# Attention with two expert layers: GpSimd carries the pairwise sums of raw keys and values one step further

## The chip, the cores and the metric

The kernel runs on one core of a Trainium2 chip. The metric is the device time of one execution in microseconds (us); the kernel before took 1105.7 us (median of 3 runs, 1105.57 to 1106.48). Lower is better. The engines are TensorE (PE), VectorE (DVE), ScalarE (ACT), GpSimd (POOL) and SyncE (SP), which here only issues transfers.

## The reference, cut to what matters

```python
# q, k, v: (8 batches, 8 heads, 576 rows, 64), float32
k_p = k.reshape(B, H, 72, 8, D).mean(axis=3)        # eight raw rows -> one
v_p = v.reshape(B, H, 72, 8, D).mean(axis=3)
scores = (q @ k_p.transpose(0, 1, 3, 2)) / sqrt(D)
attn = softmax(scores)
x = (attn @ v_p)                                     # 4608 tokens x 512
x = moe(x, w_gate, w_output_gate, w1, w2)            # 8 experts, best one per token
x = moe2(x, modality_id, w_gate, modality_bias, w1, w2)
```

The part that the change touches is the mean over eight raw rows of keys and of values, of which each batch has one tensor apiece.

## The kernel before

The 4608 tokens are worked off in 36 tiles of 128. A batch has 576 tokens, so a tile takes in the end of one batch and the start of the next now and then. The attention stage fills the first 170 us of the span; the two expert stages behind it take the rest, and the change leaves them alone.

Raw keys (or values) of a batch lie on chip as eight planes of 128 partitions x 288 numbers, where plane p holds the p-th of each eight rows. They come in two transfers of four planes, each into one buffer of a ring of seven (`ring`, names kv0 to kv6). The sum of the eight planes is built as a tree, in three places:

- `half` (L304): on GpSimd, for each of the two buffers, two additions of one plane each (L307, 128x288), which leave two planes per buffer.
- `both` (L311): on VectorE, one addition of two planes to two planes (L313, 128x576), and one of the two planes left (L315, 128x288). Behind L313 the second buffer goes back to the ring.
- `spread` (L317): ScalarE copies the sum, scaled, into the layout that the matmuls read (L327: KB for keys, VT for values). Then the first buffer goes back.

The first batch is summed on VectorE in a way of its own. In iteration i of the tile loop the program issues, engine by engine: eviction of the transposed weights of tile i-2 (`stage_et_evict`, L408, ScalarE); scores of tile i (L380, PE); the products with the values for tile i-2 (`stage_av`, L417, PE, into pav); row maxima of tile i (L385, VectorE) and their exponentials (L392, ScalarE); one entry of `lasts`, that is a `both` or a `spread`; `normalise` of tile i-2 (L431 to L438, VectorE, which reads pav); transposes of tile i-1 (L401, PE). Between these VectorE takes single steps of a list `fill` (L471 to L488): the choice of experts for a finished group of four tiles, many short instructions on 128x32 numbers or fewer, most with two inputs on chip. Twelve such steps more (L128 to L139) follow once the fourth group is through. GpSimd's work is put in order by `gp_work` (L497 and L307): each call takes one `half`, if its transfers have been issued, and one scatter of a finished tile to DRAM. Each engine works its instructions off in the order of the program.

There is one buffer of pav, so the products of the next tile wait for `normalise` of the one before. The transfers are issued on SP in the order of the program (`ldq`); one that finds no free buffer at build time makes the program issue an open sum first (`advance`), and at run time it waits for the last reader of its buffer.

Of the kernel before, what the change touches and what calls it, by code (L numbers as in the profile page):

```python
# [14 lines left out]
ALU = mybir.AluOpType  # L15
AX = mybir.AxisListType
# [26 lines left out]
SCALE = 1.0 / (8.0 * POOL)  # L43
# [4 lines left out]
def kernel(ctx, tc, q, k, v, wg, wo, w1, w2, mod, wg2, bias2, v1, v2, out):  # L48
    nc = tc.nc
    PE, ACT, DVE, GP, SP = nc.tensor, nc.scalar, nc.vector, nc.gpsimd, nc.sync  # L50
# [220 lines left out]
    KB = [pa.tile([P, NG, 2, SP_], F32, name=f"KB{i}", bufs=1) for i in range(3)]  # L271
    VB = [pa.tile([CB, NB, 2 * VW], F32, name=f"VB{i}", bufs=1) for i in range(3)]
    VT = [pa.tile([P, NG, 2, SP_], F32, name=f"VT{i}", bufs=1) for i in range(2)]
# [5 lines left out]
    qT, kR, vR = {}, {}, {}  # L279
# [19 lines left out]
                    SP.dma_start(t[lo], src[b, :, lo:lo + 4])  # L299
                ldq.append((tag, load))  # L300

    def pool_sum(eng, first, raw, dst, scale):
        def half(lo, eng):
            r = raw[lo]  # L304
            if eng is GP:
                for j in range(2):
                    GP.tensor_tensor(r[:, j], r[:, j], r[:, 2 + j], op=ALU.add)  # L307
            else:
                eng.tensor_tensor(r[:, 0:2], r[:, 0:2], r[:, 2:4], op=ALU.add)

        def both():  # L311

            DVE.tensor_tensor(raw[0][:, 0:2], raw[0][:, 0:2], raw[4][:, 0:2], op=ALU.add)  # L313
            ring.append(raw[4])
            DVE.tensor_tensor(raw[0][:, 2], raw[0][:, 0], raw[0][:, 1], op=ALU.add)  # L315

        def spread():  # L317
            apart_heads(dst, raw[0][:, 2], slice(0, NG), scale)
            ring.append(raw[0])

        return [lambda: half(0, first), lambda: half(4, eng)], [both, spread]

    def apart_heads(dst, x, gs, scale):

        for r in range(2):
            h = slice(64 * r, 64 * r + 64)
            ACT.activation(dst[h, gs, r, :], x[h].rearrange("p (g s) -> p g s", s=SP_), AF.Copy, scale=scale)  # L327

    def sum_k(b, eng):
        return pool_sum(eng, eng, kR.pop(b), KB[b % 3], SCALE)  # L330

    def sum_v(b, eng, first=None):
        return pool_sum(eng, first or eng, vR.pop(b), VT[b % 2], 1.0)

    def prep_v(b, a, name="pv"):
        t = VT[b % 2].rearrange("p g r s -> p (g r s)")
# [7 lines left out]
    def cols(T):  # L344
        t0, r0, res = T * P, 0, []
        while r0 < P:
            b = (t0 + r0) // S
            s0 = (t0 + r0) % S
            n = min(P - r0, S - s0)
            res.append((b, s0, r0, n))  # L350
            r0 += n
        return res
# [152 lines left out]
    ring = [kp.tile([P, 4, KW], F32, name=f"kv{i}") for i in range(KV)]  # L505
# [14 lines left out]
    def prefetch(b):  # L520
        load_kv(b)
        for tag, (f, l) in ((b, sum_k(b, GP)), (b + 0.1, sum_v(b, GP))):
            sums.extend((tag, g) for g in f)
            lasts.extend((tag, g) for g in l)
# [60 lines left out]
    for i in range(3):  # L585
        o = VB[i].rearrange("p (a j) (r c) -> p a j r c", a=2, r=2)
# [19 lines left out]
    kR.pop(0)  # L606
    ring.extend(k0)
    v0 = [f for fs in sum_v(0, DVE, GP) for f in fs]
    v0.pop(0)()

# [14 lines left out]
    late, vbs = [], []  # L625
# [36 lines left out]
    for i in range(NT + 1):  # L662
# [76 lines left out]
        if i + 2 < NT:  # L739
            b = cols(i + 2)[-1][0]  # L740
# [470 lines left out]
```

## Time and profile before

| what | value |
|---|---|
| median of 3 runs | 1105.7 us (1105.57 to 1106.48) |
| the profiled execution's own time | 1104.66 us |
| its span | 1103.0 us |
| granted TensorE clock, mean | 0.993 |
| busy over the span | PE 97%, DVE 54%, ACT 36%, POOL 29% |

The profiled execution is one more run; its trace covers 1103.0 us of its 1104.66 us. A busy share over the whole span mixes the attention stage, where VectorE and ScalarE are busy most of the time, with the expert stages, where they are not. For this change only the first 170 us are to be read.

### The profile page before, as it was taken

To read this page: it belongs to the slowest core of one execution; us is meant where nothing else is said; L and a number is where in the kernel's file an instruction comes from. 1 tells how busy PE (TensorE), PEld (TensorE's weight loads), DVE (VectorE), ACT (ScalarE), POOL (GpSimd) and SP (SyncE) were. 2 spreads that over 40 slices of the span, in tenths; PEclk is the share of its full clock that TensorE was granted. 3 is DMA by queue.
4 is the path that set the end of the run, shared out by engine and by line. 5 is a ranking of instruction groups with operands and counts; after the bars stand their busy time and mean duration, and the time that the engine had idled before them with its cause. 6 is when DMAs were issued, how large, how long until landed. Compare 5 with 4: busy or idle time off the path is not lost. (4 is left out here: it accounts for less than half of the span.)

```text
span 1103.0 us, 21979 instructions
## 1 busy us (share of the span) xinstructions
PE 1066.7 (97%) x7058; PEld 962.2 (87%) x7058; DVE 594.2 (54%) x1845; ACT 393.4 (36%) x924; POOL 324.9 (29%) x551
## 2 busy tenths in 40 slices
PE   7998989999999999999999999999999999999997
PEld 6998878998889888888898887988899889998886
DVE  6889777767888668669766685121111221121111
ACT  6887882215455125235312251121111332221121
POOL 7666485112847214316611111001010050000010
PEclk9999999999999999999999999999999999999999
DMA  9877455613737213316250013711111111111000
GB/s 346 283 279 259 176 178 216 216 55 109 249 131 244 77 49 135 104 40 193 76 186 24 22 42 138 240 49 43 56 50 40 41 52 48 40 40 41 30 30 23
DMA packets 52099, 128.20 MB, mean 116 GB/s; under 512 B 6957, under 2 KB 10029, under 8 KB 51760
## 3 DMA queue, kind: packets, MB, share of 16 engines
q1 hardware_dynamic: 42928, 97.28, 26.9%
q0 software_dynamic: 8960, 28.47, 6.6%
q8 instruction: 89, 1.46, 0.6%
q14 instruction: 122, 1.00, 0.3%
HBM read 92.51 MB, written 34.27 MB: 115 GB/s over the span
## 5 line engine op out<-in xcount | busy, mean ns | idle before, releaser
L773 DVE SCALAR_TENSOR_TENSOR hl<-h,hh 128x512 fp32r<-128x512 f32 x140 | 95.3, 690 | 367.5 <-ACT hh L772 365.2
L827 PE MATMUL y<-W2H,hh 128*128 128x512 f32 x608 | 234.3, 398 | 2.1 <-ACT hh L772 1.5
L827 PE MATMUL y<-W2L,hh 128*128 128x512 f32 x608 | 233.9, 395 | 0.5 <-POOL W2L L841 0.5
L827 PE MATMUL y<-W2H,hl 128*128 128x512 f32 x608 | 232.4, 395 | 0.0
L772 ACT ACTIVATE hh<-h 128x512 fp32r<-128x512 f32 x140 | 83.2, 596 | 308.0 <-PE h L783 304.5
L850 DVE CUSTOM_DVE_ANT_0 junk<-y,wg2b 128x512 f32<-128x512 f32 x273 | 169.5, 685 | 8.3 <-ACTq L1054 5.1
L830 ACT ACTIVATE y<-y,xg 128x512 f32<-128x512 f32 x76 | 52.3, 688 | 303.4 <-PE y L827 224.1
L1075 POOL DMA_INDIRECT out_dram<-y,ti x37 | 36.0, 972 | 381.4 <-ACT y L830 259.3
L827 PEld LDWEIGHTS y<-W2H,hh 128*128 128x128 f32 x608 | 114.1, 189 | 27.8 <-ACT hh L772 1.7
L827 PEld LDWEIGHTS y<-W2H,hl 128*128 128x128 f32 x608 | 114.5, 188 | 26.7
L827 PEld LDWEIGHTS y<-W2L,hh 128*128 128x128 f32 x608 | 114.6, 189 | 25.9 <-POOL W2L L841 1.3
L783 PE MATMUL h<-xH,W1L 128*128 128x256 f32 x608 | 123.0, 284 | 0.0
L841 POOL TENSOR_TENSOR W2L<-R,W2H 128x256 fp32r<-128x256 f32 x128 | 91.8, 753 | 78.7 <-ACT W2H L1056 76.9
L904 POOL DMA_INDIRECT xs<-y,qdi x39 | 39.8, 1021 | 218.5 <-DVE lg L850 160.6
L783 PE MATMUL h<-x2H,W1L 128*128 128x256 f32 x512 | 103.6, 284 | 0.0
L783 PE MATMUL h<-xH,W1H 128*128 128x256 f32 x608 | 100.2, 288 | 1.3 <-ACTq L1054 0.8
L783 PE MATMUL h<-xL,W1H 128*128 128x256 f32 x608 | 98.2, 284 | 0.0
L783 PEld LDWEIGHTS h<-xH,W1L 128*128 128x128 f32 x608 | 95.3, 193 | 0.0
L783 PEld LDWEIGHTS h<-xH,W1H 128*128 128x128 f32 x608 | 84.4, 193 | 1.7 <-ACTq L1054 1.2
L783 PE MATMUL h<-x2H,W1H 128*128 128x256 f32 x512 | 84.5, 287 | 0.4 <-ACT x2H L245 0.4
L783 PEld LDWEIGHTS h<-xL,W1H 128*128 128x128 f32 x608 | 84.3, 193 | 0.0
L783 PE MATMUL h<-x2L,W1H 128*128 128x256 f32 x512 | 83.0, 284 | 0.3 <-DVE x2L L252 0.2
(240 smaller groups left out, 1596.3 us busy)
## 6 DMA issues: line engine op xcount, KB each, us to landing
R<-in_w_dram SPq DMA_DIRECT2D x56, 512.0 KB, 5.1
xg<-xs SPq DMA_DIRECT2D x72, 258.0 KB, 2.7
kv<-in_v_dram SPq DMA_DIRECT2D x16, 576.0 KB, 5.8
R<-in_v_dram SPq DMA_DIRECT2D x16, 512.0 KB, 8.5
kv<-in_k_dram SPq DMA_DIRECT2D x14, 576.0 KB, 6.7
qt<-in_q_dram SPq DMA_DIRECT2D x14, 576.0 KB, 9.0
xs<-dummy SPq DMA_DIRECT2D x18, 258.0 KB, 2.7
wraw<-in_w_dram SPq DMA_DIRECT2D x8, 512.0 KB, 4.1
```

Of the source, the lines that this page charges most:

```text
L772: ACT.activation(HH[kk], p, AF.Relu)
L773: DVE.scalar_tensor_tensor(HL[kk], in0=p, scalar=0.0, in1=HH[kk].bitcast(F32), op0=ALU.max, op1=ALU.subtract)
L783: PE.matmul(p[:, c2, :], lhsT=W[d][:, c:c + P], rhs=x[:, d, :], start=n == 0, stop=n == 3 * ND - 1)
L827: PE.matmul(p, lhsT=X[f // 2][:, f % 2, hf * P:(hf + 1) * P], rhs=W[f // 2][:, f % 2, :], start=i == 0, stop=i == 3 * NF - 1)
L830: ACT.activation(S["y"][:, hf, 0:DM], p, AF.Copy, scale=S["xg"][:, hf, DM:DM + 1])
L841: GP.tensor_tensor(W2L[j][:, c, w], R2[j][:, c, w], W2H[j][:, c, w].bitcast(F32), op=ALU.subtract)
L850: DVE.tensor_tensor_reduce(out=M["junk"][:, e % 2], in0=p, in1=M["wg2b"][:, e, :], scale=1.0, scalar=0.0, op0=ALU.mult, op1=ALU.add, accum ...
L904: apart("xs2", GP.indirect_dma_start(xs2, IDX(ap=di[:, hf:hf + 1], axis=0), y[:, hf, :], None, bounds_check=E * REG - 1, oob_is_err=False))
L1075: apart("out", GP.indirect_dma_start(out, IDX(ap=S["ti"][:, hf:hf + 1], axis=0), S["y"][:, hf, 0:DM], None, bounds_check=N - 1, oob_is_err ...
```

## The change

From the third batch on (`late`, b > 1), GpSimd adds the second buffer's four planes into planes 2 and 3 of the first buffer, and then adds planes 2 and 3 to planes 0 and 1: six additions of 128x288 for a tensor instead of four. VectorE sums the two planes left by one `tensor_reduce` over a view in which the two numbers to be added stand side by side (they lie 288 numbers apart), instead of two `tensor_tensor`. For the first two batches the additions stay as they were, but the second buffer's result is written into the first buffer too. For all batches the second buffer goes back to the ring behind `half`, no longer behind `both`, so the ring hands out other buffers, and at one place a `both` that the program had to issue early is now issued later.

```diff
--- before.py
+++ after.py
@@ -299,19 +299,26 @@
                     SP.dma_start(t[lo], src[b, :, lo:lo + 4])
                 ldq.append((tag, load))
 
-    def pool_sum(eng, first, raw, dst, scale):
+    def pool_sum(eng, first, raw, dst, scale, late):
         def half(lo, eng):
-            r = raw[lo]
+            r, o = raw[lo], raw[0][:, lo // 2:lo // 2 + 2]
             if eng is GP:
                 for j in range(2):
-                    GP.tensor_tensor(r[:, j], r[:, j], r[:, 2 + j], op=ALU.add)
+                    GP.tensor_tensor(o[:, j], r[:, j], r[:, 2 + j], op=ALU.add)
             else:
-                eng.tensor_tensor(r[:, 0:2], r[:, 0:2], r[:, 2:4], op=ALU.add)
+                eng.tensor_tensor(o, r[:, 0:2], r[:, 2:4], op=ALU.add)
+            if lo:
+                ring.append(r)
+                if late:
+                    for j in range(2):
+                        GP.tensor_tensor(raw[0][:, j], raw[0][:, j], raw[0][:, 2 + j], op=ALU.add)
 
         def both():
 
-            DVE.tensor_tensor(raw[0][:, 0:2], raw[0][:, 0:2], raw[4][:, 0:2], op=ALU.add)
-            ring.append(raw[4])
+            if late:
+                DVE.tensor_reduce(raw[0][:, 2], raw[0][:, 0:2].rearrange("p j c -> p c j"), axis=AX.X, op=ALU.add)
+                return
+            DVE.tensor_tensor(raw[0][:, 0:2], raw[0][:, 0:2], raw[0][:, 2:4], op=ALU.add)
             DVE.tensor_tensor(raw[0][:, 2], raw[0][:, 0], raw[0][:, 1], op=ALU.add)
 
         def spread():
@@ -327,10 +334,10 @@
             ACT.activation(dst[h, gs, r, :], x[h].rearrange("p (g s) -> p g s", s=SP_), AF.Copy, scale=scale)
 
     def sum_k(b, eng):
-        return pool_sum(eng, eng, kR.pop(b), KB[b % 3], SCALE)
+        return pool_sum(eng, eng, kR.pop(b), KB[b % 3], SCALE, b > 1)
 
     def sum_v(b, eng, first=None):
-        return pool_sum(eng, first or eng, vR.pop(b), VT[b % 2], 1.0)
+        return pool_sum(eng, first or eng, vR.pop(b), VT[b % 2], 1.0, b > 1)
 
     def prep_v(b, a, name="pv"):
         t = VT[b % 2].rearrange("p g r s -> p (g r s)")
```

On VectorE, in the third and fourth iteration: nm are the row maxima, rs to lgs are `normalise`, kv_198 is the buffer with the second batch's keys. Before:

```order
L385 TENSOR_REDUCE nm_389<-ps_373 128x4
L313 TENSOR_TENSOR kv_198<-kv_198,kv_199 128x576
L315 TENSOR_TENSOR kv_198<-kv_198 128x288
L431 TENSOR_SCALAR rs<-pav 128x8
L433 RECIPROCAL rs<-rs 128x8
L435 TENSOR_TENSOR x<-pav,rs 128x512
L436 TENSOR_TENSOR ll<-pav,rs 128x128
L438 TENSOR_REDUCE lgs<-ll 128x16
L385 TENSOR_REDUCE nm_444<-ps_431 128x4
```

The same place after the change (its line numbers are 7 or 8 higher):

```order
L392 TENSOR_REDUCE nm_389<-ps_373 128x4
L438 TENSOR_SCALAR rs<-pav 128x8
L440 RECIPROCAL rs<-rs 128x8
L442 TENSOR_TENSOR x<-pav,rs 128x512
L443 TENSOR_TENSOR ll<-pav,rs 128x128
L445 TENSOR_REDUCE lgs<-ll 128x16
L321 TENSOR_TENSOR kv_198<-kv_198 128x576
L322 TENSOR_TENSOR kv_198<-kv_198 128x288
L392 TENSOR_REDUCE nm_446<-ps_433 128x4
```

The sum of the second batch's keys stands behind the first `normalise` now, and right ahead of the next row maxima.

On VectorE at the sum of the seventh batch's keys, among the twelve steps on the expert counts (fe to ford). Before:

```order
L385 TENSOR_REDUCE nm_1624<-ps_1607 128x4
L132 TENSOR_SCALAR feh_308<-rev,fm_307 128x8
L313 TENSOR_TENSOR kv_195<-kv_195,kv_194 128x576
L315 TENSOR_TENSOR kv_195<-kv_195 128x288
L133 TENSOR_TENSOR ft_309<-feh_308,ev 128x8
L431 TENSOR_SCALAR rs<-pav 128x8
L134 TENSOR_REDUCE fef_310<-ft_309 128x1
```

After:

```order
L392 TENSOR_REDUCE nm_1636<-ps_1619 128x4
L132 TENSOR_SCALAR feh_308<-rev,fm_307 128x8
L319 TENSOR_REDUCE kv_198<-kv_198 128x288
L133 TENSOR_TENSOR ft_309<-feh_308,ev 128x8
L438 TENSOR_SCALAR rs<-pav 128x8
L134 TENSOR_REDUCE fef_310<-ft_309 128x1
```

Two instructions have become one, at the same place in the row.

On GpSimd around the sums of the sixth batch, where xs is the scatter of a finished tile and each row of sums is two additions. Before:

```order
L307 TENSOR_TENSOR kv_198<-kv_198 128x288 x2
L497 DMA xs_66<-x,rdi 37888x516
L307 TENSOR_TENSOR kv_197<-kv_197 128x288 x2
L497 DMA xs_66<-x,rdi 37888x516
L427 COPY x<-meta 128x4x3
L307 TENSOR_TENSOR kv_200<-kv_200 128x288 x2
L307 TENSOR_TENSOR kv_199<-kv_199 128x288 x2
L497 DMA xs_66<-x,rdi 37888x516 x2
```

After:

```order
L307 TENSOR_TENSOR kv_194<-kv_194 128x288 x2
L504 DMA xs_66<-x,rdi 37888x516
L307 TENSOR_TENSOR kv_194<-kv_199 128x288 x2
L314 TENSOR_TENSOR kv_194<-kv_194 128x288 x2
L504 DMA xs_66<-x,rdi 37888x516
L434 COPY x<-meta 128x4x3
L307 TENSOR_TENSOR kv_196<-kv_196 128x288 x2
L307 TENSOR_TENSOR kv_196<-kv_197 128x288 x2
L314 TENSOR_TENSOR kv_196<-kv_196 128x288 x2
L504 DMA xs_66<-x,rdi 37888x516 x2
```

Two more additions stand in one run behind each second `half`: runs of two become runs of four, and the run of four for the values becomes one of six.

## Rows read from the trace of the kernel before

**Rows 1.** Windows: us, busy of each engine (instructions), clock, DMA share, GB/s.

```profile
20.00:96.00 76.00, 73.29 (x594) 69.74 (x594) 65.70 (x210) 61.15 (x222) 47.26 (x58) 1.00 0.84 301
96.00:126.00 30.00, 24.77 (x202) 22.91 (x201) 27.86 (x88) 20.75 (x76) 15.50 (x20) 1.00 0.65 221
```

**Rows 2.** Waits of PE, 30 to 126 us: total us, times, longest.

```profile
PE pav L417 <- DVE ll L436: 3.2, 2, 1.8
PE pav L417 <- ACT et L408: 1.9, 6, 0.6
PE pav L417 <- DVE ra L477: 1.1, 1, 1.1
```

**Rows 3.** Timeline of PE: start, us, what, [idle before <-releaser].

```profile
102.40 1.89 PE L417 MATMUL pav<-VB,et 96*128 96x162 f32 x12 [1.76 <-DVE ll L436]
...
121.06 1.89 PE L417 MATMUL pav<-VB,et 96*128 96x162 f32 x12 [1.45 <-DVE ll L436]
```

**Rows 4.** Timeline of VectorE at three of the sums.

```profile
81.30 0.75 DVE L313 TENSOR_TENSOR kv<-kv,kv 128x576 f32<-128x576 f32 x1
82.08 0.46 DVE L315 TENSOR_TENSOR kv<-kv 128x288 f32<-128x288 f32 x1
82.85 0.17 DVE L431 TENSOR_SCALAR rs<-pav 128x8 f32<-128x8 f32 x1 [0.31 <-PE pav L417]
...
98.06 0.77 DVE L313 TENSOR_TENSOR kv<-kv,kv 128x576 f32<-128x576 f32 x1
98.87 2.08 DVE L315 TENSOR_TENSOR kv<-kv 128x288 f32<-128x288 f32 x1
...
117.73 1.95 DVE L315 TENSOR_TENSOR kv<-kv 128x288 f32<-128x288 f32 x1
```

**Rows 5.** Timeline of GpSimd beside two of these sums.

```profile
99.06 1.56 POOL L307 TENSOR_TENSOR kv<-kv 128x288 f32<-128x288 f32 x2
...
117.80 1.56 POOL L307 TENSOR_TENSOR kv<-kv 128x288 f32<-128x288 f32 x2
```

**Rows 6.** Windows of line L313, then of L315: us, DVE busy (instructions), rest as above.

```profile
30.00:127.00 97.00, 10.12 (x12) 1.00 0.75 263
...
30.00:127.00 97.00, 10.03 (x12) 1.00 0.75 263
```

**Rows 7.** Line L313 there: ns min/median/max, first and last start.

```profile
L313 DVE TENSOR_TENSOR kv<-kv,kv x12: 746/753/1401, 32.5 to 125.4; 128x576 f32<-128x576 f32 x12
```

**Rows 8.** Two reductions on VectorE from SBUF: ns min/median/max, starts, form.

```profile
L438 DVE TENSOR_REDUCE lgs<-ll x36: 354/370/378, 22.7 to 171.8; 128x16 f32<-128x128 f32 x36
...
L161 DVE TENSOR_REDUCE tc<-tbig x2: 302/302/303, 180.1 to 671.2; 128x8 f32<-128x144 f32 x2
```

**Rows 9.** Timelines of PE, VectorE and ScalarE, 19 to 26 us.

```profile
19.13 1.82 PE L417 MATMUL pav<-VB,et 96*128 96x162 f32 x12
...
25.34 2.02 PE L380 MATMUL ps<-KB,qt 128*64 128x144 f32 x16
...
21.40 0.15 DVE L431 TENSOR_SCALAR rs<-pav 128x8 f32<-128x8 f32 x1
...
23.03 0.81 DVE L385 TENSOR_REDUCE nm<-ps 128x4 f32<-128x288 f32 x2
...
23.57 1.80 ACT L392 ACTIVATE ee<-ps,nm 128x72 f32<-128x72 f32 x8 [1.39 <-DVE nm L385]
```

**Rows 10.** Timelines of VectorE and GpSimd at two short steps of the choice.

```profile
77.17 0.15 DVE L483 SCALAR_TENSOR_TENSOR rw<-rss,rez 128x4 f32<-128x4 f32 x1
...
145.87 4.02 DVE L483 SCALAR_TENSOR_TENSOR rw<-rss,rez 128x4 f32<-128x4 f32 x1
...
72.42 3.85 POOL L307 TENSOR_TENSOR kv<-kv 128x288 f32<-128x288 f32 x4
...
144.34 2.77 POOL L640 TENSOR_TENSOR W1L<-wraw,W1H 128x256 fp32r<-128x256 f32 x4
147.09 2.79 POOL L640 TENSOR_TENSOR W2L<-wraw,W2H 128x256 fp32r<-128x256 f32 x4
```

## Prediction

> **What bounds the kernel now.** First I read the windows, because the busy shares of the whole span hide the stage that is changed. From 20 to 96 us PE is busy for 73.3 of 76 us and VectorE for 65.7; from 96 to 126 us PE falls to 24.8 of 30 and VectorE rises to 27.9 [rows 1]. So PE sets the pace of the tiles in the first stretch, with little left over, and in the second PE waits and VectorE is the engine to look at. The end of the span plays no part: the expert stages start when the attention stage is through, so what is gained or lost before 126 us should arrive at the end nearly whole.
>
> Next, the waits of PE between 30 and 126 us, all before the products with the values: 3.2 us for `normalise`, in two waits; 1.9 us for ScalarE's eviction, in six; 1.1 us for a step of the choice of experts [rows 2]. That is 6.2 us, the most that a faster VectorE could give back. The timeline of PE shows the two long ones, 1.76 us at 102.4 and 1.45 us at 121.1 [rows 3].
>
> Then VectorE at the sums. Undisturbed, L313 takes 0.75 and L315 0.46 us, and VectorE is idle for 0.31 us behind them [rows 4]. At 98.87 and 117.73 the same L315 takes 2.08 and 1.95 us, and GpSimd starts two additions right then, at 99.06 and 117.80, of 1.56 us together; both times L315 ends only after them [rows 4, 5]. These two stretched sums lie ahead of the two long waits of PE. That is what the change can remove.
>
> **The change part by part.**
>
> *Two additions become one reduction.* In the stretch that holds the twelve late sums L313 takes 10.12 and L315 10.03 us, together 20.15 [rows 6]. How long the reduction takes no row shows. It reads 576 numbers. The additions give a slope of (751 - 459)/288, about 1.01 ns a number (0.75 and 0.46 us in rows 4), and the reduction at L161, over 144 adjacent numbers, takes 302 ns [rows 8], so its fixed part is 302 - 145 = 157 ns. Read as adjacent numbers, 576 would take 157 + 582, 0.74 us: the lower end. But the new view jumps 288 numbers between the two that it adds. The one reduction that also jumps is L438, 128 numbers into 16 results: by this formula 286 ns, by the row 370 [rows 8]. If the extra 84 ns belong to the 128 reads (0.66 ns each), the new one takes 0.74 + 0.38 = 1.12 us. If they belong to the 16 results (5.2 ns each), 288 results cost 1.5 us and it takes 2.25 us: the upper end. L161 has eight results and no such excess against L438's sixteen, so I take the reads, 1.12 us. Twelve of them are 13.4 us, 6.7 us less than now.
>
> The Trainium skill has a rule against the new form: "SBUF — State Buffer", section "Door 1: The DMA port swizzle", says that an access which crosses to another 16-byte line pays a penalty. It gives no size; L438's 84 ns agree with it. By that rule the twelve cost 13.4 us and save 6.7; without it they would cost 8.9 us and save 11.3.
>
> *What this is worth on the path.* A shorter sum counts only where PE waits for VectorE. At the seventh batch's keys 2.81 us (98.06 to 100.87) become 1.12: 1.7 us earlier, against a wait of 1.76. Some of it comes back, since twelve short steps of the expert counts stand around this place and GpSimd now runs four additions there; I take 1.3 us. The 1.1 us wait behind it hangs on the choice's steps; 0.3 of it. At the eighth batch's keys 2.70 us (0.75 + 1.95) become 1.12; the wait of 1.45 us goes whole. Of the 1.9 us that PE waits for ScalarE, which itself follows VectorE's maxima, about a quarter should go, 0.5. The other sums are covered: where L313 and L315 are undisturbed VectorE is idle behind them and PE is not waiting. Together 1.3 + 0.3 + 1.45 + 0.5 = 3.55 us. Next late is PE itself.
>
> *Twelve times two more additions on GpSimd.* At 1.56/2 = 0.78 us each [rows 5], 24 additions cost 18.7 us of GpSimd. They lie beside everything, since GpSimd waits for VectorE before its scatters, and the sums are ready early: the last pair ends at 119.4 [rows 5], with two more additions at 120.9, and VectorE wants it at 125.4 [rows 7]. If the cover went, a late sum would hold VectorE, and behind it `normalise` and PE, by at most 1.56 us. Queued behind the additions on GpSimd are the scatters; nobody waits for them before the first gathered block. What is not free is that VectorE's short steps with two inputs on chip meet more additions. In the fifth and sixth batch the run of additions for the values grows and reaches steps that it missed: one such run ended at 76.27 (72.42 + 3.85), the step at 77.17 took 0.15 us [rows 10], and with four more additions ahead of its end the run now lasts to about 78.6 (3.1 us more, less some 0.75 in which the additions were held up by VectorE's). I take 0.4 us on the path for such meetings; the bounds are 0 and the price in the second rival.
>
> *Earlier release of the second buffer.* The ring hands out other buffers. Loads wait for GpSimd's first sums in the second and third batch, for VectorE's before; from then on they go out earlier. As the transfers are busy at a share of 0.84 from 20 to 96 us [rows 1], and no engine that PE waits for stands behind them, I cost it at nothing, with 0.5 us either way.
>
> *The moved sum of the second batch's keys.* It stood ahead of the first `normalise` and now stands behind it, ahead of the next row maxima. `normalise` ran from 21.40 to 23.03, 1.63 us, though its products were done at 20.95 (19.13 + 1.82). Now it starts at 20.95 and ends at 22.58, the sum takes 1.21 us, and the maxima start at 23.8 and not at 23.03. ScalarE's exponentials waited for these maxima for 1.39 us, and the scores at 25.34, stretched to 2.02 us, need keys that ScalarE writes behind them [rows 9]. So 0.75 us are lost, on the path; I take 0.7.
>
> Sum: -3.55 + 0.4 + 0.7 = -2.45 us. Against the profiled execution's own time, 1104.66, that is 1102.2 us; the profiled one lies 1.04 us under the median of the runs shown, so against 1105.7 it is 1103.3 us.
>
> **The rivals.**
>
> *Everything closes.* The reduction takes 0.74 us, the sum moved early costs nothing, and most of the 6.2 us of PE's waits go, some 5 us: 1100.7 us. For it: none of L438's 36 is stretched beyond 378 ns [rows 8], though GpSimd is busy for 47.3 of 76 us beside many of them [rows 1]. Against it: the excess of L438, and that ScalarE, for which PE waits too, has work of its own.
>
> *The wait moves to the short steps.* At 145.87 a step that takes 0.15 us elsewhere takes 4.02, until the eight additions in a row on GpSimd (144.34 to 149.88) are over [rows 10]: VectorE does not always get in between two of them. With runs of four and six additions a meeting can cost 2 to 3 us instead of 0.5. One such on the path, beside a few short ones, eats 2 us of the gain: 1105.3 us, no change. For it: both long waits of L315 lasted through a whole run too [rows 4, 5]. Against it: L313, which also reads two inputs on chip, never took more than 1.40 us [rows 7], well under the length of a run. The Trainium skill ("SBUF — State Buffer", "Who interferes with whom") says that the loser waits until the first instruction has finished, and that a reduction never contends on this chip. By this rule a meeting would cost at most 0.78 us and this rival would be worth 0.5; the 4.02 us disagree with it.
>
> *The reduction is slow.* At 2.25 us each the eight undisturbed sums become 1.04 us longer, with 0.31 us of idle behind them; the four disturbed ones gain next to nothing. From about 1.5 us (1.21 + 0.31) the reduction decides: then the maxima of the next tile, the exponentials and the eviction come late. Eight times (1.04 - 0.31) is 5.8 us; PE's order has some give, so half of it, 2.9 us, less 1 us still won at 98 and 117 us, plus 0.7 and 0.4: about 2.5 to 3 us slower, 1108 us. For it: L438's excess can be read by results. Against it: L161.
>
> **How the numbers follow.** A measurement of this kernel tells 0.2%, 2.2 us, from no change. I give the forecast 0.55, spread from 1101.5 to 1104.6 (under 1103.5 in 0.42, above in 0.13); everything closes 0.12; the wait that moves 0.20 (0.02 of it slower); the slow reduction 0.13 (0.03 within). So faster 0.54, same 0.34, slower 0.12. The range, 1101.0 to 1106.0, takes in the forecast and the moved wait, and leaves out the slow reduction and half of the first rival.
>
> **What would show it.** The profile of the changed kernel should have twelve reductions near 1.1 us, none above 1.2, whatever GpSimd does; PE's waits at about 102 and 121 us gone; 24 more additions of 128x288 on GpSimd; and the scores near 25 to 28 us later by about 0.7 us. I am wrong if the reductions are above 1.5 us, if a short step on VectorE takes over 2 us between 30 and 126 us, or if PE's waits before the products stay near 6 us in total.

## The result, and the profile after

The changed kernel took 1119.37 us (median of 4 runs, 1116.91 to 1120.5), the kernel before 1105.63 us beside it (4 runs): ratio 1.0122, 95% interval 1.0109 to 1.0136. It is 13.7 us slower. The forecast was 1103.3 us, so even its sign was wrong. The profiled execution of the changed kernel took 1120.48 us, its span 1118.8.

Windows of the changed kernel, columns as in [rows 1]:

```profile
20.00:96.00 76.00, 67.82 (x495) 63.65 (x494) 58.97 (x163) 51.37 (x185) 49.10 (x66) 0.89 0.73 259
96.00:126.00 30.00, 24.89 (x176) 22.83 (x175) 26.51 (x79) 18.85 (x66) 21.71 (x28) 0.93 0.56 203
```

From 20 to 96 us TensorE works off 495 matmuls in place of 594, and its granted clock is 0.89 in place of 1.00. So the loss lies where the forecast saw least to do. The waits of PE, 30 to 126 us (total us, times, longest):

```profile
PE ps L387 <- ACT ee L399: 8.2, 6, 3.8
PE pav L424 <- DVE ll L443: 2.2, 2, 1.8
PE pav L424 <- DVE ra L484: 0.9, 1, 0.9
```

The waits for `normalise` have fallen from 3.2 to 2.2 us and that for ScalarE's eviction is off the list of its matmuls (TensorE's weight loads still wait 4.3 us for it), but a new one of 8.2 us is there, the scores for the exponentials, which [rows 2] do not have. Its longest part is early. PE, then VectorE, then GpSimd of the changed kernel there:

```profile
40.95 0.76 PE L387 MATMUL ps<-KB,qt 128*128 128x144 f32 x4 [0.96 <-ACT ee L399]
45.49 1.33 PE L387 MATMUL ps<-KB,qt 128*128 128x144 f32 x4 [3.78 <-ACT ee L399]
...
36.65 2.83 DVE L479 TENSOR_TENSOR rd<-lgs,rm 128x32 f32<-128x32 f32 x1
39.40 0.45 DVE L392 TENSOR_REDUCE nm<-ps 128x4 f32<-128x288 f32 x1
39.77 4.31 DVE L480 SCALAR_TENSOR_TENSOR ra<-rd,rev 128x32 f32<-128x32 f32 x1
44.01 0.45 DVE L392 TENSOR_REDUCE nm<-ps 128x4 f32<-128x288 f32 x1
...
25.68 3.20 POOL L307 TENSOR_TENSOR kv<-kv 128x288 f32<-128x288 f32 x4 [3.83 <-DMA kv<-in_k_dram]
...
34.85 3.06 POOL L307 TENSOR_TENSOR kv<-kv 128x288 f32<-128x288 f32 x4
37.86 1.55 POOL L314 TENSOR_TENSOR kv<-kv 128x288 f32<-128x288 f32 x2
39.35 0.20 POOL L434 COPY x<-meta 128x12 f32<-128x12 f32 x1
39.49 3.04 POOL L307 TENSOR_TENSOR kv<-kv 128x288 f32<-128x288 f32 x4
42.48 1.55 POOL L314 TENSOR_TENSOR kv<-kv 128x288 f32<-128x288 f32 x2
```

Read it from below. GpSimd has two runs of additions here. The first ends with the six from 34.85 to 39.41; twelve more stand ahead of these without a gap, from 25.68 us on, where the kernel before paused for 2.77 us ahead of 34.36. The second has six, 39.49 to 44.03. Two short steps of the choice of experts on VectorE (L479 and L480) start inside the first and at the head of the second, and each lasts until its run is over. The two halves of the row maxima (L392) stand behind them, so the exponentials come late, and the scores behind those stand for 3.78 us. Later steps are held to the end of a run in the same way: 2.63 us at 68.73, 1.51 at 80.57, 2.18 at 99.66, 1.82 at 112.87.

What follows shows in windows of 4 us, columns as in [rows 1]:

```profile
40.00:44.00 4.00, 0.76 (x4) 0.54 (x4) 4.00 (x1) 0.90 (x4) 4.00 (x6) 0.88 0.71 279
44.00:48.00 4.00, 2.46 (x8) 2.12 (x9) 3.89 (x15) 3.48 (x14) 0.03 (x1) 0.50 0.23 32
48.00:52.00 4.00, 4.00 (x22) 3.79 (x21) 1.39 (x5) 1.50 (x7) 0.00 (x0) 0.50 0.66 263
52.00:56.00 4.00, 4.00 (x28) 3.99 (x28) 2.07 (x12) 2.70 (x11) 0.00 (x0) 0.84 0.30 51
56.00:60.00 4.00, 4.00 (x33) 3.93 (x32) 3.65 (x11) 3.45 (x13) 2.58 (x3) 1.00 1.03 407
```

TensorE was busy for 0.76 us of the first window; behind it the granted clock is 0.50, its lower level (1.2 GHz), through two windows, though PE is busy for all of the second of these, and it comes back behind them. The clock falls again at 76 to 80 us (0.50), 104 to 108 us (0.57) and 128 to 132 us (0.53).

The rows that answer to [rows 7] and to the two new additions (ns min/median/max, first and last start):

```profile
L319 DVE TENSOR_REDUCE kv<-kv x12: 745/752/765, 33.4 to 144.2; 128x288 f32<-128x576 f32 x12
L314 POOL TENSOR_TENSOR kv<-kv x24: 778/789/803, 28.8 to 139.9; 128x288 f32<-128x288 f32 x24
```

The reduction is faster than forecast and never stretched: its own time cannot be what made the kernel slower.

### The profile page after: what moved, and what is told of

It is laid out like the page before. It is cut to its first block, busy times and chain, and to the rows that moved or that the text cites. A ratio compares the mean times of both kernels' runs of the same rounds, so it can differ in the third digit from the quotient of the medians.

```text
span 1118.8 us, 21988 instructions
## 1 busy us (share of the span) xinstructions
PE 1078.7 (96%) x7058; PEld 972.4 (87%) x7058; DVE 597.7 (53%) x1833; ACT 394.9 (35%) x924; POOL 340.4 (30%) x575
```

## The experiments

Unless told otherwise an edit is to the changed kernel. The table has, for each kernel, its median, its ratio to the runs of before beside it (95% interval), and how much later than in the kernel before `normalise` of tiles 4, 12, 22 and 35 starts in the profiled executions (us, from VectorE's timelines). The first tile's `normalise` is up to 1.6 us later than in the kernel before even where the edit acts only behind it (cover, stalls), so small differences in these columns mean nothing. Code that is left out is marked `...`.

| kernel | us | ratio | 4 | 12 | 22 | 35 |
|---|---|---|---|---|---|---|
| changed | 1119.37 | 1.0122 (1.0109 to 1.0136) | 6.4 | 13.4 | 20.3 | 17.8 |
| ring_only | 1104.71 | 0.9998 (0.9989 to 1.0008) | 1.0 | 0.9 | 1.5 | -0.1 |
| more_adds | 1106.02 | 1.0011 (1.0000 to 1.0022) | 0.2 | 0.8 | 3.1 | 1.9 |
| more_memsets | 1107.06 | 1.0027 (1.0014 to 1.0039) | 0.8 | 3.2 | 2.7 | 1.4 |
| broken_runs | 1109.67 | 1.0049 (1.0033 to 1.0066) | 1.0 | 5.1 | 7.2 | 5.4 |
| adds6_tt | 1110.95 | 1.0057 (1.0040 to 1.0074) | 2.7 | 7.8 | 12.1 | 9.8 |
| reduce4 | 1103.9 | 1.0002 (0.9991 to 1.0012) | 0.6 | 1.1 | 0.9 | -0.8 |
| late_b4 | 1111.88 | 1.0064 (1.0047 to 1.0081) | 0.9 | 8.7 | 10.9 | 8.3 |
| cover | 1115.51 | 1.0084 (1.0054 to 1.0113) | 7.2 | 11.1 | 12.8 | 10.3 |
| pm_after | 1101.8 | 0.9976 (0.9964 to 0.9989) | 1.4 | 0.4 | 2.2 | -1.6 |
| pm_before | 1101.9 | 0.9978 (0.9968 to 0.9988) | 0.2 | -0.4 | -0.6 | -2.4 |
| reduce4_adds | 1107.06 | 1.0035 (1.0017 to 1.0053) | 0.5 | 8.9 | 11.7 | 10.0 |
| stalls | 1120.93 | 1.0145 (1.0128 to 1.0162) | 6.5 | 12.3 | 17.9 | 17.3 |
| pm_first | 1108.45 | 1.0032 (1.0020 to 1.0045) | 1.1 | 3.8 | 4.7 | 2.5 |
| pm_reduce4 | 1104.44 | 0.9993 (0.9984 to 1.0003) | 0.4 | 0.6 | 1.1 | -1.7 |

**ring_only**: no late batch, so the ring, the early release and the moved sum alone.

```diff
-        return pool_sum(eng, eng, kR.pop(b), KB[b % 3], SCALE, b > 1)
+        return pool_sum(eng, eng, kR.pop(b), KB[b % 3], SCALE, False)   # and so in sum_v
```

> The additions and VectorE's two sums stay as before for all batches; only the second half's target plane, the earlier release of the buffer and the moved sum of the second batch's keys are taken from the change. Theory (starved short steps: VectorE's short steps with two inputs on chip wait for the end of a run of GpSimd additions, and the longer runs cost the time): within 2 us of before, 1104 to 1108 us. Rival (order: the ring and the moved sum are the loss): 1115 to 1120 us.

No difference. Tile 4 is 1.0 us later, as the moved sum has it in the changed kernel too, and it is won back by tile 35. The two steps of the first group that the changed kernel holds start inside runs of GpSimd here too, runs of four, and get in (VectorE, GpSimd):

```profile
36.63 0.26 DVE L479 TENSOR_TENSOR rd<-lgs,rm 128x32 f32<-128x32 f32 x1
...
37.17 0.46 DVE L480 SCALAR_TENSOR_TENSOR ra<-rd,rev 128x32 f32<-128x32 f32 x1
...
34.34 3.24 POOL L307 TENSOR_TENSOR kv<-kv 128x288 f32<-128x288 f32 x4 [2.46 <-DMA kv<-in_k_dram]
```

**more_adds** (the kernel before, with two additions over dead planes behind each late second half) and **more_memsets** (three clears there instead):

```diff
+                if lo and late:
+                    for j in range(2):
+                        GP.tensor_tensor(r[:, 2 + j], r[:, 2 + j], r[:, 2 + j], op=ALU.add)
+                    # more_memsets: for j in range(3): GP.memset(r[:, 2:4], 0.0)
```

> The kernel before, with two more additions on GpSimd behind each second half of the late batches, over planes that nobody reads any more. VectorE's work, the ring and all orders are those of before. Theory (starved short steps): as slow as the change or slower, 1115 to 1125 us, with short steps on VectorE of 2 us and more. Rival (order): 1105 to 1108 us. Rival (the new sums depend on GpSimd's later result): 1105 to 1108 us, as nothing waits for the added work.

> The kernel before, with three memsets of two planes (about 1.6 us together, as long as two additions) on GpSimd behind each second half of the late batches, over planes that nobody reads any more. Theory (starved short steps: it is the reading additions that hold VectorE off): within 3 us of before, 1104 to 1108 us. Rival (GpSimd's longer time, whatever it does): 1115 to 1120 us, like the additions.

A miss for more_adds, which took the time that its two rivals gave; ring_only speaks against the first of them, reduce4_adds below against the second. Longer runs alone cost 1.5 us (1106.02 - 1104.51): the additions are there, but no step of the choice or of the counts took more than 2.07 us before 126 us, and none more than 0.8 us before 71. More_memsets is within its range. There one of VectorE's sums is held, by the additions and not by the clears behind them (VectorE, GpSimd):

```profile
58.45 3.67 DVE L318 TENSOR_TENSOR kv<-kv 128x288 f32<-128x288 f32 x1
...
58.77 3.03 POOL L307 TENSOR_TENSOR kv<-kv 128x288 f32<-128x288 f32 x4
61.87 1.85 POOL L310 MEMSET kv<- 128x576 f32 x3
```

It ends at 62.12, when the four additions are over and the clears, to 63.72, have begun.

**broken_runs**: a clear of 64 numbers on a scratch tile behind each late addition.

```diff
                     GP.tensor_tensor(o[:, j], r[:, j], r[:, 2 + j], op=ALU.add)
+                    if late:
+                        GP.memset(gap, 0.0)   # likewise behind the two extra additions
```

> The change as it is, with a memset of 64 numbers on GpSimd (about 0.1 us) behind each addition of the late batches, so that no two additions follow each other directly. Theory (starved short steps, held off because the next addition starts at once): the gaps let VectorE in, its short steps stay under 1 us and the time falls to 1102 to 1108 us. Rival (GpSimd's share of the port as such): 1116 to 1121 us as before the gaps, or slower.

Two of its steps in the first group, VectorE's timeline:

```profile
36.69 0.92 DVE L482 TENSOR_TENSOR rd<-lgs,rm 128x32 f32<-128x32 f32 x1
...
39.36 0.75 DVE L487 TENSOR_TENSOR ra<-rohb,lgs 128x32 f32<-128x32 bf16 x1
```

Here VectorE waits for about one addition (0.81 us), and tile 4 is as late as in ring_only. But at 55.81 and 91.38 us steps still took 2.14 and 2.36 us, through three additions with clears between them, so a gap does not always let it in, and the time, 1109.67 us, is above the theory's range. Without the first group's long waits 5.2 us of the 13.7 are left; why a step is held or not the run does not show.

**adds6_tt** (VectorE sums the two planes by one addition) and **reduce4** (the kernel before, but one reduction over four planes, into the second buffer):

```diff
-                DVE.tensor_reduce(raw[0][:, 2], raw[0][:, 0:2].rearrange("p j c -> p c j"), axis=AX.X, op=ALU.add)
+                DVE.tensor_tensor(raw[0][:, 2], raw[0][:, 0], raw[0][:, 1], op=ALU.add)   # adds6_tt
...
+                DVE.tensor_reduce(raw[4][:, 0], raw[0].rearrange("p j c -> p c j"), axis=AX.X, op=ALU.add)   # reduce4, ahead of the two sums of before
```

> The change with its six additions on GpSimd, but VectorE adds the last two planes by one tensor_tensor (128x288, 0.46 us undisturbed) and not by the reduction (0.75 us). Theory A (the length of GpSimd's runs decides, whatever VectorE runs): 1116 to 1121 us, like the change. Theory B (VectorE's two-input sums that fall into a run break it up and hold GpSimd back, so that the short steps behind them get in; the reduction needs no port and took that away): 1104 to 1110 us, with short steps under 1.2 us.

> The kernel before with four additions on GpSimd per tensor, as it was, but for the late batches VectorE sums the last four planes by one reduction over 1152 numbers (about 0.15 + 1.2 = 1.35 us, never held up); the result lies in the second buffer, and the first goes back to the ring in its place. Theory A: runs as short as before and no two-input sum on VectorE, so the waits at 98 and 117 us go: 1100 to 1104 us. Theory B: without the two-input sums the short steps are held off to the end of GpSimd's runs, 1108 to 1118 us.

Runs of six without the reduction lose 6.7 us (1110.95 - 1104.27), the reduction without runs of six loses nothing. So adds6_tt lies between its two theories. There it is mostly the sum itself that is held, 4.05 us at 61.31 and at 81.02. The reduction of reduce4 takes 2.18 us and not the 1.35 of its expectation:

```profile
L315 DVE TENSOR_REDUCE kv<-kv x12: 2151/2184/2199, 33.0 to 125.7; 128x288 f32<-128x1152 f32 x12
```

The twelve are 26.2 us on VectorE, 6 more than the sums of before [rows 6], and the time is still the same.

**late_b4**: the change from the fifth batch on (`b > 3` for `b > 1`).

> The change, but only from the fifth batch on; the third and fourth are summed as before. The longest runs (25 to 44 us, eighteen additions and more with one short copy between) are as before then. Both theories: the waits of 2.8 and 4.3 us at 36 and 40 us and the drop of PE's clock behind them go, the later ones stay: 1109 to 1114 us. Rival (the order of the ring's buffers or something in the late stages is the loss): 1117 us and above.

It leaves one long meeting, a sum on VectorE beside GpSimd; behind these, the windows:

```profile
58.53 4.98 DVE L322 TENSOR_TENSOR kv<-kv 128x288 f32<-128x288 f32 x1
...
58.67 3.03 POOL L307 TENSOR_TENSOR kv<-kv 128x288 f32<-128x288 f32 x4
61.67 1.53 POOL L314 TENSOR_TENSOR kv<-kv 128x288 f32<-128x288 f32 x2
...
60.00:64.00 4.00, 0.85 (x7) 0.63 (x6) 3.93 (x4) 0.29 (x1) 3.19 (x5) 1.00 0.57 177
64.00:68.00 4.00, 3.11 (x12) 3.14 (x13) 2.15 (x9) 2.31 (x10) 0.00 (x0) 0.58 0.22 88
```

A sum that takes 0.46 us [rows 4] lasts as long as the whole run of six, PE stands, and the clock falls to 0.58. `normalise` of tile 8, ahead of this meeting, is 0.6 us later than in the kernel before, that of tile 11, the last ahead of the next held step (1.91 us at 76.47), 7.4: 6.8 us for a wait of 4.5.

**cover**: matmuls on a constant keep PE busy ahead of two late scores (the second half of tile 7's, the first of tile 13's).

```diff
+                n = {(7, 1): 34, (13, 0): 14}.get((i, a))
+                if n:
+                    cover = ps_a.tile([P, 2 * BLK], F32, name="pv")
+                    for _ in range(n):
+                        PE.matmul(cover[:, 0:P], lhsT=ones_b, rhs=ones_b, start=True, stop=True)
```

> The change with matmuls that nobody reads put on PE where it waits for the exponentials: 34 (some 3.7 us) between the two halves of the scores of tile 7, and 14 (1.5 us) ahead of those of tile 13. They take part of the idle time only. Theory (the falls of PE's granted clock to half, at 43 to 53 and 74 to 81 us, come from its idling and are a loss of their own, some 4 us of the 13): the clock stays at 1.00 in both stretches and the time falls to 1113 to 1117 us. Rival (the clock falls for another reason, or costs nothing, as PE isn't what binds there): 1118 to 1122 us.

The waits of VectorE are nearly those of the changed kernel (the first is 1.83 us and not 2.83, the second 4.32); the clock from 36 to 56 us is 0.91, not 0.74. Tile 35 is 10.3 us late, not 17.8; against the runs of before beside it the median is 11.2 us longer (1115.51 - 1104.27), not 13.7. So the clock seems to have a share, 2.5 to 7.5 us as this run has it. But the intervals of the two ratios touch, the first wait is 1 us shorter, and the added matmuls cost something themselves: the size stays open.

**psum_after**, **psum_before** and **psum_reduce4** (the changed kernel, the kernel before and reduce4): the short steps' operands in the free quarter of the two PSUM banks that the transposes of the exponentials use. PSUM is the memory in which PE's results lie here (ps, pav, pm); the short steps' operands lie in SBUF, the large on-chip memory, otherwise.

> The changed kernel, but the operands of the choice's short steps (logits, differences, keys of the choice, sums of exponentials) of the first eight groups lie in the free quarter of two PSUM banks and not in SBUF, so each of VectorE's two-input steps there has at most one input in SBUF. The order of the instructions is that of the changed kernel. Theory (two-input steps of VectorE wait in SBUF until GpSimd's longer rows of additions end, the maxima behind them come late, TensorE stands and its granted clock falls): 1101 to 1107 us, none of these steps over 1 us between 30 and 190 us, no window of 4 us there with a granted clock below 0.7. Rival 1 (the loss comes from something else that the reductions and the extra additions do together): 1115 to 1121 us as the changed kernel. Rival 2 (steps with both inputs, or one, in PSUM are held as well): 1113 to 1121 us with the same steps at 2 to 4 us.

1165.5, 1179.9 and 1186.4 us: all three missed. Waits of psum_after, 20 to 190 us (total us, times, longest):

```profile
PEld pe L409 <- DVE pe L450: 45.9, 23, 2.8
...
PE pe L409 <- DVE pe L450: 40.2, 23, 2.5
```

PE's transposes (L409) now wait for the logits that VectorE writes into the same bank. So these runs tell of a placement and not of the theory.

**pm_after** and **pm_before** (the same for the changed kernel and the kernel before): operands of the short steps in the bank of the rank counts (`pmt`) instead, which is free by then; the order stays. `lgs` stays in SBUF; one step takes the chosen expert from the differences, so that it too has one input in PSUM.

```diff
+        if in_ps:   # the first eight groups
+            d, dd = (pmt[:, c:c + 4 * E].rearrange("p (t e) -> p t e", t=4)[:, 0:G] for c in (96, 128))
+            m, ssum = pmt[:, 72:72 + G], pmt[:, 80:80 + G]
+        rv = rev_p if in_ps else rev
...
-            V(lambda: (mark(), DVE.tensor_tensor(ohb, c8(rev), bc(km), op=ALU.is_equal))),
-            V(lambda: DVE.tensor_tensor(a2, ohb, og, op=ALU.mult)),
+            V(lambda: (mark(), DVE.tensor_tensor(ohb, c8(rv), bc(km), op=ALU.is_equal))),
+            V(lambda: DVE.scalar_tensor_tensor(a2, in0=d, scalar=0.0, in1=og, op0=ALU.is_ge, op1=ALU.mult) if in_ps else ...),
```

> The changed kernel, but with the maximum, the differences, the sums of exponentials, the row offsets and the constant that marks the chosen expert of the first eight groups in the bank in which TensorE counts the ranks anyway, which is used at no other time by then. Each two-input step of the choice then has at most one input in SBUF, and no transposition shares a bank with it. Theory (the loss is the waiting of these steps through GpSimd's runs and what follows from it): 1101 to 1108 us, none of these steps over 1 us between 30 and 110 us, and tile 35's normalisation at most 4 us later than in the kernel before. Rival 1 (something else that the reductions and the two additions do together): 1115 to 1121 us. Rival 2 (steps with an operand in PSUM wait as well): 1113 to 1121 us, and steps of 2 to 4 us as in the changed kernel.

> The kernel before with the same operands in the bank of the ranks. Theory: its one long wait (4.02 us at 145.87) and the shorter ones go, VectorE's two-input sums stay: 1101 to 1105 us. Rival (PSUM operands and their order cost something of their own, whatever GpSimd does): 1107 us or more, and by that much pm_after would have to be read higher too.

pm_after at the same place, VectorE, GpSimd and windows:

```profile
37.12 0.20 DVE L491 TENSOR_TENSOR pm<-lgs,pm 128x32 f32<-128x32 f32 x1
...
37.59 0.18 DVE L492 SCALAR_TENSOR_TENSOR ra<-pm,rev 128x32 f32<-128x32 f32 x1
...
39.72 0.18 DVE L496 SCALAR_TENSOR_TENSOR ra<-pm,lgs 128x32 f32<-128x32 f32 x1
...
34.99 3.06 POOL L307 TENSOR_TENSOR kv<-kv 128x288 f32<-128x288 f32 x4
38.00 1.56 POOL L314 TENSOR_TENSOR kv<-kv 128x288 f32<-128x288 f32 x2
39.49 0.20 POOL L434 COPY x<-meta 128x12 f32<-128x12 f32 x1
39.64 3.06 POOL L307 TENSOR_TENSOR kv<-kv 128x288 f32<-128x288 f32 x4
...
40.00:44.00 4.00, 3.65 (x29) 3.42 (x28) 3.05 (x11) 3.07 (x12) 4.00 (x6) 1.00 0.96 365
44.00:48.00 4.00, 4.00 (x37) 3.98 (x36) 3.19 (x15) 2.93 (x11) 0.20 (x1) 1.00 0.85 274
```

GpSimd's runs stand where they stood, the steps stand in them, and none is held: 0.20, 0.18, 0.18 us. The clock stays at 1.00 up to 108 us (0.66 in the window behind). The time is 2.9 us below the runs of before beside it, where the changed kernel lies 13.7 above its own: 16.6 us. So the loss was the held steps and what they drew after them; with one operand off the SBUF they are not held. (A step of the expert counts, whose operands stay in SBUF, still takes 1.82 us at 96.55.) pm_before gains 2.8 us in the same way, so 13.8 of the 16.6 are what the change had added. pm_before and pm_after are equal: without the meetings the change is worth nothing either way, and the two are the fastest kernels here, 0.2% under the kernel before.

**reduce4_adds**: reduce4 with the two additions of more_adds, so that no reduction needs them.

> One reduction over four planes (as reduce4, which ran at 1103.9) and the two additions over dead planes behind each late second half (as more_adds, 1106.0): so GpSimd's runs and VectorE's reductions are as many and as long as in the changed kernel, but no reduction needs the two additions. Theory (runs of six additions, no two-input sum of VectorE between them that holds the short steps back to the run's end, so the short steps meet the runs): 1112 to 1121 us with steps of 2 to 4 us. Rival (the sum that comes later, as the reduction needs the additions, is what costs): 1103 to 1107 us.

Its ten runs lie between 1104.3 and 1112.7 us, wider than any other. The median is below the theory's range and at the edge of the rival's. The profiled one is the longest, and has one long wait before 150 us, at the head of a run (VectorE, GpSimd):

```profile
38.86 4.32 DVE L485 TENSOR_TENSOR ra<-rohb,lgs 128x32 f32<-128x32 bf16 x1
...
38.84 3.04 POOL L308 TENSOR_TENSOR kv<-kv 128x288 f32<-128x288 f32 x4
```

A loss of 8 us is there without any sum that waits for the two additions, so the rival falls for this execution. That its runs differ by 8 us fits a meeting that takes place in some of them and not in others; only one of them has a trace, so that is not shown.

**stalls**: the kernel before, with VectorE held by reductions of a constant at six places.

```diff
+        n = {(6, 0): 17, (6, 1): 27, (12, 0): 16, (14, 0): 8, (18, 1): 13, (21, 0): 10}.get((T, a))
+        if n:
+            hold = sm.tile([P, 32], F32, name="hold")
+            DVE.tensor_reduce(hold[:, 0:n], ident.unsqueeze(1).to_broadcast([P, n, P]), axis=AX.X, op=ALU.add)
```

> The kernel before, but VectorE is kept busy for as long as the six longest waits of the changed kernel before 115 us last (2.6, 4.1, 2.4, 1.3, 2.0 and 1.6 us, 14 us in all) at the same six places, by one-input reductions of a constant; GpSimd's additions and the sums are those of before. Theory (a stall of VectorE ahead of the maxima moves the program by about its length, as TensorE stands and its granted clock falls): 1113 to 1121 us, windows of 4 us behind the stalls with a granted clock at or below 0.8. Rival (VectorE has room to catch up, and the loss was GpSimd's lateness): 1104 to 1108 us.

The first two of these stalls on VectorE, and the windows behind them:

```profile
37.31 2.41 DVE L387 TENSOR_REDUCE hold<-ident 128x17 f32<-128x2176 f32 x1
...
40.45 3.74 DVE L387 TENSOR_REDUCE hold<-ident 128x27 f32<-128x3456 f32 x1
...
40.00:44.00 4.00, 1.24 (x9) 0.77 (x7) 4.00 (x3) 0.96 (x4) 1.23 (x2) 0.91 0.26 95
44.00:48.00 4.00, 2.36 (x8) 2.02 (x9) 3.90 (x15) 3.37 (x13) 0.00 (x0) 0.50 0.19 31
48.00:52.00 4.00, 4.00 (x22) 3.82 (x22) 1.83 (x7) 1.49 (x7) 0.00 (x0) 0.50 0.77 262
```

With GpSimd and the sums as before, six stalls, 13.0 us in all, bring back the whole loss and more (16.3 us, 1120.93 - 1104.65), and the windows read as in the changed kernel: PE idle, then 0.50.

**pm_first**: pm_after for the first group alone (`in_ps = g == 0`).

> The changed kernel with the operands of the choice in the bank of the ranks for the first group only (tiles 0 to 3), whose steps held VectorE for 2.83 and 4.31 us at 36.65 and 39.77; the other groups stay in SBUF. Theory (each meeting costs by itself): tile 4's normalisation at most 2 us later than in the kernel before (6.4 in the changed one), the later meetings find other places in GpSimd's runs and cost some of the 9 us that lie behind: 1105 to 1113 us. Rival (the waits of the first group do not matter, the loss comes back elsewhere): 1114 to 1121 us.

Tile 35 is 2.5 us late, not 17.8, and the clock is 1.00 in every window read from 36 to 190 us, though steps of about 2 us stay at 54.96, 72.50, 89.83 and 101.42. Against the runs of before beside each, the loss falls from 13.7 to 3.3 us: the first group's meeting makes 10.4 of it, with what it draws after it. There both maxima of one tile are held in a row; that this is why it costs so much is not shown.

**pm_reduce4**: reduce4 with the operands of pm_before.

> The kernel before with one reduction over four planes (reduce4, 1103.9 us, which has GpSimd's runs of four and no two-input sum on VectorE) and the operands of the choice of the first eight groups in the bank of the ranks. Theory: nothing two-input is left beside GpSimd's additions but the favourite's steps: 1099 to 1102 us, the fastest. Rival (with the short steps out of the way the sums are hidden anyway): as pm_before and pm_after, 1101 to 1103.

A miss: between 30 and 160 us no held step is left over 0.8 us, and it is not faster than pm_before. The reduction over four planes takes 2.19 us on average here too.

## Why the prediction was wrong

**The bound.** That PE sets the pace until 96 us, with little left over, was right [rows 1]. The conclusion drawn from it was the wrong way round: it was used to cost VectorE's work there at nothing, while a stretch without slack is where a wait is paid (in stalls 13.0 us of waits cost 16.3).

**The reduction.** 1.12 us were forecast, 0.752 measured, near the lower end (0.74). No jump penalty shows between pairs. For four planes the same formula gives 1.32 us (157 ns and 1152 times 1.01), and reduce4's took 2.18, so the size of a penalty stays open. By the prediction's sentence on the Trainium skill's rule ("SBUF — State Buffer", "Door 1: The DMA port swizzle") the twelve would have cost 13.4 us; they cost 9.0, the value without it.

**What it gives back** (3.55 us). The two stretched L315 did go, as forecast. But of it little came: pm_after and pm_before differ by 0.1 us, so even if the 1.0 us of the moved sum reached the end, the reductions are worth about 1 us.

**The moved sum.** 0.75 us forecast, 1.0 at tiles 1 to 3 in the changed kernel; a right step, and without effect on the end in ring_only.

**The ring.** Nothing, as forecast (ring_only).

**The step that failed:** "I take 0.4 us on the path for such meetings; the bounds are 0 and the price in the second rival." The mechanism was named, and the sign of failure too ("a short step on VectorE takes over 2 us between 30 and 126 us"), but the size was off: 0.4 us, where the change added 13.8 (pm_after gives back 16.6, pm_before 2.8). Three things were missing. It priced one meeting of 2 to 3 us; there were six over 1.5 us before 115 us, one of 2.83 and one of 4.31. It looked for them in the fifth and sixth batch, while the costliest came in the first group of tiles, at 36 to 44 us, where the trace of before has GpSimd's additions (34.36 to 40.56) and the same two steps side by side as well (VectorE, GpSimd):

```profile
35.66 0.30 DVE L472 TENSOR_TENSOR rd<-lgs,rm 128x32 f32<-128x32 f32 x1
...
36.26 0.46 DVE L473 SCALAR_TENSOR_TENSOR ra<-rd,rev 128x32 f32<-128x32 f32 x1
...
34.36 3.06 POOL L307 TENSOR_TENSOR kv<-kv 128x288 f32<-128x288 f32 x4 [2.77 <-DMA kv<-in_k_dram]
```

And it took a meeting to cost its own length, though the clock falls behind it: 4.5 us of wait in late_b4 became 6.8.

**The rivals.** "The wait moves to the short steps" was the right one, with too small a price: its reason against ("L313 ... never took more than 1.40 us") told of the meetings of L313 alone. The row that spoke for it, 4.02 us at 145.87 [rows 10], was a fair sample of what was to come. "The reduction is slow" had the right sign for a reason that the runs refute; "everything closes" had the reduction's time (0.74 us), and the rest of it did not come.

**What stays open.** Why a step that starts inside a run gets in after one addition in one kernel (0.26 and 0.46 us in ring_only) and waits to the end of the run in another. Many of the long waits started at the head of a run (39.77, 38.86, 58.53), but 36.65 and 68.73 did not. The length of a run does not decide it: in more_adds and adds6_tt the additions stand without a gap from 25.4 and 25.6 us too, and the same two steps took 0.32 and 0.46 us there, and 0.40 and 0.46. These two kernels have VectorE's two-input sums among the runs, the changed one has reductions; that this makes the difference is a guess. So that a meeting would happen at 36 us could hardly be foretold; that it could cost 4 us could.

## What to carry to other kernels

Where one engine has no slack, take as the bound of a possible wait the longest that the trace shows (here 4.02 us) times the number of places where it can happen, and not the usual one, and add what the standing engine's clock takes afterwards. Before lengthening back-to-back runs of two-input work on GpSimd, give the short two-input steps of VectorE beside them one operand in PSUM, in a bank that no other engine needs at that time; here that took out every long wait of these steps and made the kernel before 0.2% faster by itself. A sum of times on an engine off the critical path (18.9 us more on GpSimd, 11.1 fewer on VectorE) told nothing of the result.

## What the runs showed of the hardware

- A VectorE instruction with both inputs in SBUF can be held through several GpSimd additions in a row, not only the current one: 4.31 us through six (39.49 to 44.03), 4.98 us for a sum of 0.46 through the six from 58.67 to 63.20 (late_b4). Clears on GpSimd did not hold one (more_memsets, 61.87 to 63.72). The Trainium skill ("SBUF — State Buffer", "Who interferes with whom") says that the loser waits until the first instruction finishes; an addition takes 0.79 us here, so these rows disagree.
- With one of the two inputs in PSUM the same steps in the same runs took 0.18 to 0.20 us (pm_after), and none of the twelve reductions from SBUF in the changed kernel took more than 765 ns. Both agree with that section of the Trainium skill, by which an instruction of VectorE with at most one input in SBUF, outside its two-port modes, and a reduction do not contend with GpSimd.
- Behind the stretch in which TensorE stood for 0.96 and 3.78 us its granted clock was 0.50 from 44 to 52 us, and 1.00 again from 56 us. In stalls, with VectorE held by hand, it was 0.50 in the same two windows.
